# Input gradient of a strided convolution: even and odd positions as matmul groups in the last five chunks, shared products split once more, instruction order written out as a list

## The chip, the cores and the metric

One core of one Trainium2 chip runs the whole kernel in one launch. The metric is the device time of one execution in microseconds (us); lower is better. The core has five engines: PE (TensorE, matmuls; its weight loads are shown as PEld), DVE (VectorE), ACT (ScalarE), POOL (GpSimd) and SP (SyncE, which here issues nearly all DMAs). Each engine runs its own instructions in the order in which they are written, and waits on semaphores for the others.

## The reference

Forward: a convolution with stride 2 and 31 taps over `x` (2 x 16000 x 256), with a 256 x 256 matrix per tap, then a normalisation over time per batch and channel, scale and shift, and a GELU. The kernel returns the output and all four gradients for a given `grad_out` (2 x 7985 x 256), in bf16:

```python
s = 2
L = (T - K) // s + 1                       # 7985
h = jnp.einsum('blc,cd->bld', x[:, 0:s * L:s, :], w[0])
for i in range(1, K):
    h = h + jnp.einsum('blc,cd->bld', x[:, i:i + s * L:s, :], w[i])
mu = jnp.einsum('bld->bd', h)[:, None, :] / L
var = jnp.einsum('bld->bd', (h - mu) ** 2)[:, None, :] / L
h = (h - mu) / jnp.sqrt(var + 1e-5)
return _gelu(h * gn_gamma[None, None, :] + gn_beta[None, None, :])

_out, _vjp = jax.vjp(_f, x, w, gn_gamma, gn_beta)
return (_out, *_vjp(grad_out))
```

The change lies in the gradient with respect to `x`: the gradient `dl` of `h`, convolved with the transposed and reversed taps.

## The kernel before, in words

**Stages.** The forward convolution of the two batches (stages F0 and F1) comes first, then the input gradient (G0 and G1) with the elementwise gradient of the GELU beside it, and last the weight gradient (W). Each stage is a long stream of matmuls on PE, with bf16 operands in SBUF (one big tile, `arena`) and fp32 sums in PSUM (`ps`, eight banks, used as four pairs).

**Products saved by differences.** All three convolutions replace products by sums. Positions and taps are dealt out by their remainders; a pair of outputs that would need four block products gets by with three, one of which (on a difference or sum of inputs, with a difference or sum of taps) is shared by both outputs. This is done three times over: a branch `br` in {B, A, C} and a leaf `lf` in {B, A, C} name the two outer levels, nine leaves in all, and inside a leaf a third level shares one product between the output halves `e` = 0 and 1.

**The input gradient.** It goes through eight chunks t = 4b + c (batch b, chunk c) of 2048 positions. In a chunk DVE forms the differences on which the leaves work (`g_sums`, line 1278: `first` for the branch, `second` for its leaves A and C, `third` for the two inputs of the unshared products). PE then runs units, one for each half chunk `pr` and branch: six units to a chunk. A unit owns two PSUM pairs, `px` and `pt`:

- `g_three_b` (line 1351): the shared product of leaf B, 4 matmuls of 512 columns into one bank of `px`; ACT copies it to the other bank (line 1359).
- `g_outer` (line 1361), in the last five chunks alone (t = 3 to 7, `GO`): the shared products of leaves A and C, 4 matmuls each, into the two banks of `pt`.
- `g_three_ac` (line 1369) for leaf B: 8 matmuls added to `px`.
- `g_seed` (line 1381): ACT keeps `pt` in SBUF (`GTB`, by `keep`, line 839), and one DVE addition of 128 x 2048 (line 1393) writes the start values of both `pt` and `px`: leaf B's sum plus the shared product of A, or of C.
- `last(A)` and `last(C_)`, run during the next unit: 8 matmuls each by `g_three_ac`, and `g_evac` (line 1395), which for branches A and C adds the kept sums of branch B on DVE (line 1403) into the output tile `HO`, and for branch B keeps them on ACT (line 839). SP stores `HO` in runs of 4096 bytes.

That is 36 matmuls of 512 columns to a unit in the last five chunks. `W2DO` and `W2DC` hold the tap sums for `g_outer`; `w2_outer` forms them during t = 2.

**The gradient of h.** `e_load` (line 1199) loads two tiles of 512 KB (`dyd` and `hd`) per chunk and channel half, `e_comp` (line 1207) scales and adds them. The scaling is on DVE for t = 3, 4, 5 (lines 1214 and 1216) and on ACT for t = 6, 7 (lines 1221 and 1223), the addition on DVE (line 1225). ACT then spreads the sum over the planes of a tile `ET`, of which there are two (line 1234).

**For the weight gradient**, `dl_turn` (line 1262) transposes each of the nine leaves of a chunk by two DMA transposes from SP (line 557) into one of four small tiles `DNO`, and POOL stores them to DRAM (`dld`, line 552). `weight_grad` (line 1664) loads them back (`d_tile`), and subtracts some of them (line 1706) ahead of its first matmuls (line 1540).

**What sets the order.** The helpers do not emit; each records an operation with its engine and what it reads and writes. `Plan.order` gave every operation a due time (from a table of leads and a finer table by part), and `Plan.listing` ran a model of the engines and queues over them; the recorded operations were then emitted in the order of the model's start times (`emit`, line 461). Each engine's own program order comes from that list.

Of the kernel before, what the change touches and what calls it, by code (L numbers as in the profile page):

```python
# [38 lines left out]
class Plan:  # L39

    def __init__(self, tc):
# [7 lines left out]
        self.look = 13  # L51
        self.pads = (3122.5, 3149.5, 2842.0)
        self.lead = {
            "F0 f_evac last": 5.0,
            "F0 f_mm f_leaf": -288.0,
            "F0 f_mm f_outer": -149.5,
            "F0 f_mm f_three_ac": -4.5,
            "F0 f_mm f_three_b": -5.5,
            "F0 f_mm pe_turn": -527.0,
            "F0 f_outer forward": -46.0,  # L60
            "F0 f_seed forward": -48.5,
            "F0 f_three_b forward": -129.5,
            "F0 keep f_evac": 35.5,
            "F0 load conv_stem_kernel": -15.5,
            "F0 load f_evac": 42.5,
            "F0 tt f_sums": -120.5,
            "F0 tt second": 20.5,
            "F0 tt third": -36.0,
            "F0 turn w2_part": -3.0,
            "F0 turn x_load": -8.5,  # L70
            "F0 ve f_seed": -122.5,
            "F0 ve_neg f_seed": 49.0,
            "F0 w_sub f_first": -76.5,
            "F0 w_sum w2_part": -13.5,
            "F1 f_evac last": -106.5,
            "F1 f_mm f_leaf": -335.0,
            "F1 f_mm f_outer": 74.0,
            "F1 f_mm f_three_ac": -8.5,
            "F1 f_mm f_three_b": -75.5,
            "F1 f_three_b forward": -73.0,  # L80
            "F1 gelu_unit gelu_batch": -2.0,
            "F1 load gelu_unit": 23.0,
            "F1 load out0_store": 15.0,
            "F1 tt f_sums": -79.5,
            "F1 tt gelu_unit": -49.5,
            "F1 tt second": -38.0,
            "F1 tt third": -225.5,
            "F1 turn gelu_batch": 56.0,
            "F1 turn gelu_unit": -12.5,
            "F1 turn x_load": 35.5,  # L90
            "F1 w_sub f_again": 4.5,
            "G0 e_comp e_load": 0.5,
            "G0 g_evac last": 1.5,
            "G0 g_mm g_leaf": -24.5,
            "G0 g_mm g_outer": 22.0,
            "G0 g_mm g_three_ac": -0.5,
            "G0 g_mm g_three_b": -7.0,
            "G0 g_three_b input_grad": 4.5,
            "G0 gelu_unit gelu_batch": -7.0,
            "G0 keep g_evac": -281.0,  # L100
            "G0 keep g_seed": -15.0,
            "G0 load dl_turn": 2.5,
            "G0 load e_load": 41.0,
            "G0 load g_evac": 23.5,
            "G0 load gelu_unit": -7.0,
            "G0 spread e_comp": -1.0,
            "G0 tiny elem_finalize": -1.0,
            "G0 tt first": -111.5,
            "G0 tt second": -4.5,
            "G0 tt third": -12.5,  # L110
            "G0 turn dl_turn": 3.5,
            "G0 turn gelu_batch": -12.0,
            "G0 w_sum load_w2": -53.0,
            "G0 w_sum w2_outer": -11.5,
            "G1 cp e_comp": 7.0,
            "G1 e_comp e_load": 12.0,
            "G1 g_mm g_outer": -15.0,
            "G1 g_mm g_three_ac": -8.5,
            "G1 g_mm g_three_b": -35.0,
            "G1 g_seed input_grad": 8.5,  # L120
            "G1 g_three_b input_grad": -11.0,
            "G1 keep g_evac": -1.0,
            "G1 keep g_seed": -108.5,
            "G1 load dl_turn": 11.0,
            "G1 load e_load": -6.0,
            "G1 load g_evac": 14.5,
            "G1 spread e_comp": -5.5,
            "G1 tt second": -16.0,
            "G1 tt third": -128.0,
            "G1 turn dl_turn": 4.0,  # L130
            "G1 zero e_comp": -6.0,
            "W keep w_keep": -3.0,
            "W keep weight_grad": -12.5,
            "W leaf_d weight_grad": 0.5,
            "W load d_tile": -54.0,
            "W load out0_late": 115.0,
            "W load w_done": -7.5,
            "W load w_emit": 28.0,
            "W load weight_grad": 2.0,
            "W load x_more": -9.0,  # L140
            "W load x_raw": 1.0,
            "W pair_d weight_grad": 1.5,
            "W pair_x weight_grad": 1.5,
            "W turn out0_late": -21.0,
            "W ve w_done": -11.0,
            "W ve weight_grad": -25.0,
            "W w_add weight_grad": 2.5,
            "W w_add x_more": 1.5,
            "W w_add x_tile": 29.5,
            "W w_both weight_grad": 11.0,  # L150
            "W w_emit w_done": 13.0,
            "W w_emit weight_grad": -261.0,
            "W w_mm w_leaf": -10.0,
            "W w_pairs weight_grad": -112.5,
        }
        self.spare = {k + " dl_turn": 3.0 for k in ("G0 turn", "G0 load", "G1 turn", "G1 load")}
        self.room, self.mixed = 2048.0, 2.2
        self.overlap = {"DVE": 0.084, "ACT": 0.1}
        self.fine = {
            "F0 f_evac last": {0: -191.0, 1: -57.0, 3: -4.0},  # L160
            "F0 f_mm f_outer": {0: 138.5, 2: 14.0},
            "F0 f_mm f_three_ac": {0: -41.0, 1: -74.0, 2: -68.0, 3: -25.5},
            "F0 f_mm f_three_b": {2: 96.5, 3: 55.0},
            "F0 f_mm pe_turn": {0: -106.0},
            "F0 f_outer forward": {0: 69.5},
            "F0 f_seed forward": {0: -15.0, 3: -58.5},
            "F0 keep f_evac": {1: -5.5, 2: -40.5, 3: -32.5},
            "F0 load f_evac": {0: -85.5, 3: 8.5},
            "F0 load put": {1: 170.5, 3: 1.0},
            "F0 load_gb conv_stem_kernel": {1: -70.0},  # L170
            "F0 tt f_sums": {1: 46.0, 3: 20.0},
            "F0 tt second": {0: 77.0, 1: -78.0, 2: 2.0, 3: -60.0},
            "F0 tt third": {0: 60.5, 1: -127.0, 2: 39.0, 3: -34.5},
            "F0 turn w2_part": {1: 3.0, 3: -18.0},
            "F0 turn x_load": {0: 87.0, 1: 94.0, 3: 29.5},
            "F0 ve_neg f_seed": {0: 232.5, 2: 9.0},
            "F0 w_sub f_first": {0: 132.0},
            "F0 w_sum w2_part": {0: 47.5, 1: 26.5, 2: 10.0, 3: 9.5},
            "F1 f_mm f_leaf": {1: 73.0},
            "F1 f_mm f_outer": {3: -293.5},  # L180
            "F1 f_mm f_three_ac": {3: -2.0},
            "F1 f_mm f_three_b": {3: -106.0},
            "F1 gelu_unit gelu_batch": {0: -7.0, 4: 15.5, 6: 23.5},
# [153 lines left out]
    def listing(self, due, succ):  # L337
# [14 lines left out]
        air = []  # L352
# [1516 lines left out]
```

## Time and profile before

| | before |
|---|---|
| median of 3 runs (lowest to highest) | 1144.24 us (1144.07 to 1147.97) |
| span of the profiled execution | 1144.1 us |
| PE busy | 1120.0 us, 98%, 7652 matmuls |
| PE weight loads busy | 748.4 us, 65% |
| DVE busy | 997.0 us, 87% |
| ACT busy | 530.1 us, 46% |
| POOL busy | 126.3 us, 11% |

The profile is of one execution, whose span is within 0.2 us of the median; nothing else of it lies outside the span. The tables by stretch (called windows here) give each engine's busy time between two points, counted from the span's start, the count of instructions in brackets, the mean TensorE clock that was granted (PEclk, 1.00 is full) and the mean load of the sixteen DMA engines. In timelines and groups, the bracket at the end of a row is the idle time of that engine just before it, and what ended it. Rows of `PE` are matmuls, `PEld` their weight loads, `SPq` DMAs as SP issues them.

By the lines of the matmuls, the input gradient runs from about 412 to 829 us and the weight gradient from there on; the first `g_seed` addition of the last five chunks (line 1393) begins at 595 us, the last one at 823 us.

### The profile page before, as it was taken

What the parts mean: (1) busy time and instruction counts of PE and PEld (TensorE: products, weight loads), DVE (VectorE), ACT (ScalarE), POOL (GpSimd) and SP (SyncE); (2) the same over time, 40 slices, a digit from 0 to 9 for tenths busy, and PEclk for the clock granted to TensorE, in tenths of its full rate; (3) what the DMA queues carried; (4) which work ended last, traced back from release to release, by engine and by line L of the source; (5) the groups of instructions that cost most, each with busy time, mean ns of one, the idle gap of its engine ahead of it and who ended that gap; (6) DMA issues with size and microseconds to landing.
All of it is one profiled execution on the core that took longest, in us unless ns stands there. A gap on an engine that the chain in (4) does not pass through costs nothing.

```text
span 1144.1 us, 18907 instructions
## 1 busy us (share of the span) xinstructions
PE 1120.0 (98%) x7652; PEld 748.4 (65%) x7652; DVE 997.0 (87%) x931; ACT 530.1 (46%) x814; POOL 126.3 (11%) x221
## 2 busy tenths in 40 slices
PE   6999999999999999999999989999999999999998
PEld 4888899877777874444444434444488766666785
DVE  7998787798989997999899877967799998788995
ACT  1353454768777588888744454732212212111200
POOL 0000000000000002232223233132200000000000
PEclk9999999999999999999999999999999999999999
DMA  9476657769786599999979787695898825999564
GB/s 221 76 190 114 168 159 149 169 177 203 192 213 151 198 362 263 278 302 247 236 204 242 168 193 162 198 235 140 262 322 259 292 72 200 347 332 310 181 200 130
DMA packets 348249, 243.57 MB, mean 213 GB/s; under 512 B 233819, under 2 KB 317409, under 8 KB 345985
## 3 DMA queue, kind: packets, MB, share of 16 engines
q1 hardware_dynamic: 341057, 223.47, 72.8%
q0 software_dynamic: 7104, 18.89, 6.0%
q8 instruction: 60, 0.98, 0.4%
q14 instruction: 28, 0.23, 0.1%
HBM read 106.24 MB, written 80.25 MB: 163 GB/s over the span
## 4 chain that ended last, share of the span: by engine, by line
PE 78%; DVE 12%; DMA 3%; issue 3%; ACT 2%; SPq 2%; DVEq 0%; ACTq 0%
PE ps L744 32%; PE ps L1540 25%; PE ps L1332 21%; DVE ps L1393 2%; DVE arena L1403 2%; SPq L552 1%; DVE arena L1285 1%; DVE arena L1119 1%; DVE arena L686 1%; DVE arena L702 1%; DVE arena L1225 1%; SPq L557 1%; DMA arena<-vl 1%; DMA arena<-in_x_dram 1%; DMA arena<-dyd 1%
## 5 line engine op out<-in xcount | busy, mean ns | idle before, releaser
L744 PE MATMUL ps<-arena 128*128 128x256 bf16 (+4 forms) x3460 | 407.9, 281 | 10.0 <-DMA arena<-in_x_dram 5.8
L1332 PE MATMUL ps<-arena 128*128 128x512 bf16 x1872 | 403.9, 377 | 7.8 <-ACT ps L1359 4.8
L744 PEld LDWEIGHTS <-arena 128*128 128x128 bf16 x3460 | 338.0, 98 | 79.8 <-DMA arena<-in_x_dram 6.1
L1332 PEld LDWEIGHTS <-arena 128*128 128x128 bf16 x1872 | 183.6, 98 | 227.3 <-issue 15.5
L1540 PE MATMUL ps<-arena 128*128 128x256 bf16 (+1 forms) x2320 | 308.9, 296 | 2.4 <-DVE arena L1706 1.5
L1540 PEld LDWEIGHTS <-arena 128*128 128x128 bf16 x2320 | 226.8, 98 | 84.5 <-issue 1.9
L839 ACT ACTIVATE arena<-ps 128x1024 f32<-128x1024 f32 x109 | 110.7, 1022 | 259.7 <-PE ps L1540 86.6
L702 DVE TENSOR_TENSOR arena<-arena 128x2064 bf16<-128x2064 bf16 (+8 forms) x125 | 155.4, 1268 | 31.9 <-PE ps L744 31.4
L552 POOL DMA_DIRECT2D dld<-arena x144 | 104.3, 726 | 252.4 <-DMA arena<-arena 232.4
L1119 DVE TENSOR_TENSOR arena<-arena 128x2048 bf16<-128x2048 bf16 (+1 forms) x80 | 95.7, 1196 | 8.3 <-ACT arena L1113 5.0
L1285 DVE TENSOR_TENSOR arena<-arena 128x1032 bf16<-128x1032 bf16 (+1 forms) x126 | 88.7, 726 | 8.0 <-PE ps L1332 4.1
L1393 DVE TENSOR_TENSOR ps<-ps,arena 128x2048 f32<-128x2048 f32 x30 | 68.9, 2296 | 29.0 <-PE ps L1332 17.6
L1505 DVE TENSOR_TENSOR arena<-arena 128x4096 bf16<-128x4096 bf16 (+1 forms) x50 | 87.2, 1779 | 6.0 <-DMA arena<-in_x_dram 5.8
L1403 DVE TENSOR_TENSOR arena<-ps,arena 128x1024 bf16<-128x1024 f32 x64 | 76.8, 1217 | 12.7 <-PE ps L1332 12.5
L859 ACT ACTIVATE arena<-ps 128x512 bf16<-128x512 f32 (+1 forms) x64 | 37.1, 580 | 52.6 <-PE ps L744 52.1
L1642 ACT COPY ps<-ps 128x256 f32<-128x256 f32 x54 | 19.3, 359 | 84.1 <-PE ps L1540 82.9
L561 POOL MEMSET arena<- 128x128 bf16 (+11 forms) x40 | 8.5, 243 | 430.1 <-DVE arena L702 140.0
L1359 ACT COPY ps<-ps 128x512 f32<-128x512 f32 x48 | 27.8, 580 | 41.7 <-PE ps L1332 41.7
L814 ACT ACTIVATE arena<-ps 128x512 f32<-128x512 f32 x56 | 29.7, 598 | 36.1 <-DVE ps L824 20.6
L1711 DVE TENSOR_TENSOR arena<-arena 128x4608 bf16<-128x4608 bf16 x16 | 40.6, 2556 | 4.7 <-PE ps L1540 4.7
L1626 DVE TENSOR_TENSOR arena<-arena 128x2048 bf16<-128x2048 bf16 x36 | 43.0, 1224 | 1.2 <-PE ps L1540 1.1
L780 ACT ACTIVATE ps<-ps 128x256 f32<-128x256 f32 x72 | 26.6, 370 | 32.8 <-PE ps L744 31.6
(81 smaller groups left out, 717.7 us busy)
## 6 DMA issues: line engine op xcount, KB each, us to landing
arena<-in_x_dram SPq DMA_DIRECT2D x28, 1024.0 KB
dld<-arena POOLq DMA_DIRECT2D x144, 128.0 KB, 4.0
out_dram<-arena SPq DMA_DIRECT2D x35, 512.0 KB
arena<-hd SPq DMA_DIRECT2D x32, 512.0 KB
arena<-in_x_dram SPq DMA_DIRECT2D x26, 512.0 KB
arena<-dld SPq DMA_DIRECT2D x18, 640.0 KB
arena<-dld SPq DMA_DIRECT2D x18, 576.0 KB
vl<-arena SPq DMA_DIRECT2D x36, 256.0 KB
```

The lines of the kernel that those rows point to most:

```text
L552: lambda: e.dma_start(out=out, in_=in_), dma=np_ * ns / 16e3 * 1.03, ns=ns, tp=SH[pk], slack=slack)
L702: lambda: nc.vector.tensor_tensor(out=o, in0=a, in1=b, op=ALU.add))
L744: yield nc.tensor.matmul(ps[:, dh, cs], lhsT=wt, rhs=mv, start=s0, stop=False, skip_group_check=True)
L839: lambda: nc.scalar.activation(out=out, in_=ps, func=ACT.Copy, scale=scale))
L1119: add("DVE", dve(nf), [o], [a, b_], lambda: V.tensor_tensor(out=o, in0=a, in1=b_, op=op))
L1285: lambda: nc.vector.tensor_tensor(out=o, in0=a, in1=b, op=ALU.subtract))
L1332: yield nc.tensor.matmul(ps[:, e, 0:wide], lhsT=lt, rhs=mv, start=s0, stop=False, skip_group_check=True)
L1393: lambda: nc.vector.tensor_tensor(out=o, in0=x, in1=g, op=ALU.add))
L1403: lambda: nc.vector.tensor_tensor(out=ho[:, :, k, :], in0=ps[:], in1=g, op=ALU.add))
L1505: add("DVE", dve(o.free_size()), [o], [a, b], lambda: nc.vector.tensor_tensor(out=o, in0=a, in1=b, op=ALU.add))
L1540: yield nc.tensor.matmul(ps[:, s, c0:c1], lhsT=lt, rhs=mv, start=s0, stop=False, skip_group_check=True)
L1626: add("DVE", dve(2048), [o], [u, v], lambda o=o, u=u, v=v: nc.vector.tensor_tensor(out=o, in0=u, in1=v, op=ALU.subtract))
```

## The change

**The last five chunks (t = 3 to 7) are computed in other groups.** A unit was one branch of a run of 128 neighbouring output positions (`pr`). Now it is one branch of every second position: `s` = 0 the even ones, `s` = 1 the odd ones. The weight operand of such a matmul is read with a step of two elements. The loops are now chunk, branch, `s`; before they were chunk, `pr`, branch.

**The shared products of leaves A and C are split a fourth time.** With the two taps w0 and w1 of a shared product and its input P, the even positions need P[2k] w1 + P[2k+1] w0 and the odd ones P[2k+1] w1 + P[2k+2] w0. `g_common` computes P[2k+1] (w0 + w1) once for both (2 matmuls a leaf, with the new tap sums `W4`), ACT keeps it in SBUF (`GTM`), and for the odd positions ACT writes it back to PSUM; `g_apart` adds the difference P[2k] - P[2k+1], or P[2k+1] - P[2k+2], times one tap (2 matmuls a leaf and `s`; one of the taps is negated beforehand). The differences are one new DVE operation per chunk and branch (`fourth`). For a chunk and branch this is 4 + 8 matmuls where `g_outer` had 16.

**What goes with it.** `g_seed` makes two DVE additions of 128 x 1024 in place of one of 128 x 2048. The gradient of h is written straight into planes (`EP`, `P3`): for t = 4 to 7 it is loaded in four quarters of 256 KB per tile through one pair of buffers (`EGP`), scaled on ACT and added on DVE by two instructions; the ACT copies of `e_comp` are gone there. `EP` and the branch tiles `SA` and `SC` exist once. `DNO` has three tiles for these chunks, not four. The transposes of a branch's leaves follow that branch, so those of branch C come last. The output is stored for each branch and `s`, in runs of 1024 bytes.

**The order is a list.** `Plan.order`, `Plan.listing` and their tables are gone; `SEQUENCE` names all 3414 recorded operations in the order in which they are emitted. It is another order in all stages, the forward and the weight gradient among them, whose operations are the same as before.

```diff
+SEQUENCE = (
+    1, 9, 11, 0, 3, 12, 2, 10, 21, 13, 4, 5, 8, 14, 7, 6, 15, 16, 37, 33, 34, 40, 30, 31,
...
+)
...
     def emit(self):
         pin = self.tc.keep_in_program_order
-        for i in self.order():
...
+        for i in SEQUENCE:
...
+    EP, P3 = sb(182016, 3, 2, 2, EM), [sb(o, 2, 2, EM) for o in (165376, 188224)]
+    EGP = [sb(o, 4, HM) for o in (86016, 88064)]
...
     def e_load(b, c):
+        if 4 * b + c > 2:
+            e_planes(b, c)
+            return
...
+    def e_planes(b, c):
...
+        for dh in range(2):
...
+            for e in range(2):
+                eg, eh = (v[:, e] for v in EGH[dh]) if t == 3 else EGP
+                gv, hv = (v.rearrange("p k f -> p (k f)") for v in (eg, eh))
+                if t > 3:
+                    for v, d in ((hv, h_d[b][c]), (gv, dy_d[b][c])):
+                        load(v, d[:, 2048 * dh + 1024 * e:2048 * dh + 1024 * e + 1024], 1 << 18, 2048, "SP")
+                e_scale(t, gv, hv, s4, s5, s6)
+                o, i = EP[:, :, dh, e, 2:2 + wd], [v[:, 1:4, 0:wd] for v in (eg, eh)]
+                e_add(o, *i)
+                w3 = wd + (wd < HM and e == 0)
+                o = p3[:, dh, 1 - e, 1 + e:1 + e + w3]
+                e_add(o, eg[:, 0, 0:w3], eh[:, 0, 0:w3])
...
+        def fourth(br):
+            v = GLS[place(br)][:, :, :, 1]
+            tt(GDE[:, :, :, 0:257], v[:, :, :, 0:257], v[:, :, :, 1:258])
...
+    def step_of(s):
+        return lambda q: slice(s + q, s + q + 2 * P - 1, 2)
...
+    def g_common(pt, br, pl, lf):
+
+        w4, k = W4[MIR[br], MIR[lf]], 0 if lf == A else 1
+        jobs = [(k, 512, pl[1][:, dh, 1:2 * P:2], w4[:, dh, :], dh == 0) for dh in range(2)]
+        g_mm(pt, jobs, [pt[:, k]], [w4, pl[1]])
+
+    def g_apart(pt, br, lf, s):
+
+        wd, k = (W2DO if lf == A else W2DC)[MIR[br]], 0 if lf == A else 1
+        jobs = [(k, 512, GDE[:, k, dh, s:s + 2 * P - 1:2], wd[:, dh, 1 - s, :], False) for dh in range(2)]
+        g_mm(pt, jobs, [pt[:, k]], [wd[:, :, 1 - s], GDE[:, k], pt[:, k]])
...
         keep(GTB.rearrange("p k f -> p (k f)"), flat2(pt))
...
-        add("DVE", dve(2048, 1), [pt[:], px[:]], [px[:], GTB],
-            lambda: nc.vector.tensor_tensor(out=o, in0=x, in1=g, op=ALU.add))
+        for k, ps in ((0, pt), (1, px)):
...
+            add("DVE", dve(1024, 1), [ps[:]], [px[:], GTB[:, k]],
+                lambda ps=ps, g=g: nc.vector.tensor_tensor(out=ps[:], in0=px[:], in1=g, op=ALU.add))
...
+        for t in range(3, 8):
...
+            for br in ORDER:
+                for s in range(2):
+                    at = step_of(s)
+                    px, pt = slots4(i)
+                    if s == 0:
+                        us = {B_: third(br, B_)}
+                    g_three_b(px, br, B_, planes(br, B_), at)
+                    if s == 0:
+                        second(br, A)
+                        second(br, C_)
+                        fourth(br)
+                    if s == 0:
+                        for lf in (A, C_):
+                            g_common(pt, br, planes(br, lf), lf)
+                    last(A)
...
+                    if s == 0:
+                        keep(GTM.rearrange("p k f -> p (k f)"), flat2(pt))
+                    else:
+                        keep(flat2(pt), GTM.rearrange("p k f -> p (k f)"))
+                    for lf in (A, C_):
+                        g_apart(pt, br, lf, s)
+                    g_three_ac(px, br, B_, us[B_], at)
...
+                        last(C_)
+                    if s == 0:
+                        us[A], us[C_] = third(br, A), third(br, C_)
+                    g_seed(px, pt, True)
...
-        if (pr, br) == (1, B_):
+        if 4 * b + c < 3 and (pr, br) == (1, B_):
             dl_turn(b, c, leaf)
+        if 4 * b + c > 2 and pr == 0:
+            dl_turn(b, c, leaf, (br,))
```

**Where instructions stand now.** ACT, before, where the gradient of the third chunk of batch 1 (t = 6) is loaded. Line 1359 copies a leaf B product, line 839 keeps a PSUM pair in SBUF, lines 1221 and 1223 scale a 512 KB load of `hd` and of `dyd`, line 1234 spreads the sum:

```order
L839 ACTIVATE arena<-ps 128x1024 x3
L1359 COPY ps<-ps 128x512
L1223 ACTIVATE arena<-arena,stats 128x1024 x2
L1221 ACTIVATE arena<-arena,stats 128x1024 x2
L1359 COPY ps<-ps 128x512
L839 ACTIVATE arena<-ps 128x1024
L1234 COPY arena<-arena 128x3x256 x2
L1234 COPY arena<-arena 128x256 x2
L839 ACTIVATE arena<-ps 128x1024 x2
```

And ACT now, where that of the second chunk of batch 1 (t = 5) is loaded. Line 1264 is the copy of a leaf B product, line 643 is `keep` (`arena<-ps` keeps a PSUM pair, `ps<-arena` writes `GTM` back), lines 1062 and 1064 scale a 256 KB load of `hd` and of `dyd`:

```order
L643 ACTIVATE arena<-ps 128x1024 x3
L1062 ACTIVATE arena<-arena,stats 128x1024
L1064 ACTIVATE arena<-arena,stats 128x1024
L643 ACTIVATE arena<-ps 128x1024 x2
L643 ACTIVATE ps<-arena 128x1024
L1264 COPY ps<-ps 128x512
L643 ACTIVATE arena<-ps 128x1024
L1264 COPY ps<-ps 128x512
L1062 ACTIVATE arena<-arena,stats 128x1024
L643 ACTIVATE arena<-ps 128x1024
```

The scalings of a 512 KB pair of loads stood together, four in a row; now those of each 256 KB pair stand apart, twice as often, with the writes of `GTM` between them.

SP, before, at the end of the input gradient. `in_x_dram` and `dld` are loads for the weight gradient, the transposes are those of `dl_turn`, `out_dram` are stores:

```order
L557 DMA_TRANSPOSE arena<-arena 128x4x128 x11
L552 DMA arena<-in_x_dram 128x8x512 x2
L552 DMA arena<-dld_0_80 128x2304
L557 DMA_TRANSPOSE arena<-arena 128x4x128 x2
L552 DMA out_dram<-arena 128x2048 x2
L552 DMA arena<-dld_0_89 128x2304
L552 DMA arena<-dld_0_80 128x2560
L552 DMA arena<-dld_0_89 128x2560
```

And SP now, at the same place (line 349 is the transpose, line 344 any other DMA):

```order
L349 DMA_TRANSPOSE arena<-arena 128x4x128 x4
L344 DMA out_dram<-arena 116x4x512
L349 DMA_TRANSPOSE arena<-arena 128x4x128
L344 DMA arena<-dld_2_82 128x2560
L349 DMA_TRANSPOSE arena<-arena 128x4x128
L344 DMA out_dram<-arena 116x4x512
L349 DMA_TRANSPOSE arena<-arena 128x4x128
L344 DMA arena<-dld_0_89 128x2560
L349 DMA_TRANSPOSE arena<-arena 128x4x128
L344 DMA arena<-dld_0_89 128x2304
```

In the list before, all but two of the last chunk's transposes are issued ahead of the first `dld` loads. In the new list the last four transposes shown stand singly between these loads and the last stores. `dld_0_89` holds transposed leaves of batch 1 for the first matmuls of the weight gradient.

More of the change, by code (lines that the diff above doesn't have):

```diff
@@ L50, in __init__ @@
         self.hold = -1
[L51 to L155, printed above, removed]
@@ L461, in emit @@
     def emit(self):
         pin = self.tc.keep_in_program_order
[L463 removed]
+        place = {i: k for k, i in enumerate(SEQUENCE)}
+        assert len(place) == len(self.ops)
+        assert all(place[p] < place[i] for i, o in enumerate(self.ops) for p in o["preds"])
+        for i in SEQUENCE:
             r = self.ops[i]["fn"]()
@@ L1243, in e_comp, with e_add, e_edge @@
+    def e_add(o, a, b_):
+        add("DVE", dve(o.free_size()), [o], [a, b_], lambda: nc.vector.tensor_tensor(out=o, in0=a, in1=b_, op=ALU.add))
+    def e_edge(b, c):
+        et = ET[(4 * b + c) % 2]
         if c == 0:
```

540 lines of the change are left out of this document (190 added, 350 removed), and 145 rows, old and new, of tables (MIR, SEQUENCE).

## The prediction

> **What bounds the kernel now.** I read the page's totals first, then the chain that ended last.
>
> ```profile
> span 1144.1 us, 18907 instructions
> ...
> PE 1120.0 (98%) x7652; PEld 748.4 (65%) x7652; DVE 997.0 (87%) x931; ACT 530.1 (46%) x814; POOL 126.3 (11%) x221
> ...
> PE 78%; DVE 12%; DMA 3%; issue 3%; ACT 2%; SPq 2%; DVEq 0%; ACTq 0%
> ```
>
> PE is busy for 98% of the span, so only fewer matmuls or fewer gaps can shorten it. A table of windows, cut at the stages and at PE's gaps, says where the 24.1 us without a matmul are (us, PE, PEld, DVE, ACT, POOL with counts, granted clock, DMA load, GB/s).
>
> ```profile
> 41.00:408.00 367.00, 366.54 (x3130) 305.53 (x3128) 320.53 (x313) 222.03 (x401) 5.54 (x14) 1.00 0.72 176
> 408.00:590.00 182.00, 179.25 (x893) 87.17 (x891) 168.05 (x193) 146.58 (x186) 47.09 (x77) 1.00 1.01 270
> 590.00:660.00 70.00, 67.50 (x312) 30.33 (x310) 64.14 (x77) 30.12 (x41) 21.11 (x34) 1.00 0.85 205
> 660.00:670.00 10.00, 8.02 (x30) 3.33 (x30) 6.80 (x5) 6.00 (x9) 6.02 (x9) 0.83 1.05 173
> 670.00:822.00 152.00, 151.82 (x710) 69.24 (x709) 115.64 (x104) 64.22 (x78) 42.20 (x70) 1.00 0.75 192
> 822.00:850.00 28.00, 25.81 (x205) 19.92 (x204) 28.00 (x26) 4.29 (x9) 1.44 (x2) 1.00 1.06 362
> 850.00:1140.30 290.30, 289.69 (x2149) 209.80 (x2147) 259.22 (x184) 49.65 (x80) 0.53 (x1) 1.00 0.73 233
> ```
>
> The last five chunks of the input gradient, which the change rewrites, fill 590 to 822. From 670 on PE is busy for 151.82 of 152 us: there a matmul that goes takes its full time out of the span, unless a new wait puts it back. The one bad spot is 660 to 670, with 30 matmuls in 10 us and a granted clock of 0.83. Of the 24.1 us, 13.4 lie at the start and the end of the program. The forward stage (41 to 408) loses 0.46 us, the weight gradient (850 on) 0.6 us. Another order has nothing to win there; I count it at 0, with 1.5 us to either side.
>
> The sum is made against the profiled execution, 1144.1 us, which is the median (1144.24) within 0.2.
>
> **Part by part: fewer matmuls.** The price of one matmul of 512 columns is read from a stretch of PE's timeline without a gap.
>
> ```profile
> 779.71 21.99 PE L1332 MATMUL ps<-arena 128*128 128x512 bf16 x102
> ```
>
> 21.99 / 102 = 0.2156 us. For each chunk and branch `g_outer` had 16 matmuls, `g_common` and `g_apart` have 4 + 8 = 12. Five chunks, three branches: 15 x 4 = 60 matmuls fewer, 1080 become 1020. Check: 1080 x 0.2156 = 232.8 us, and the windows from 590 to 822 are 232. So -60 x 0.2156 = **-12.9 us**. The Trainium skill's "TensorE: Matmul & The Clock Gate" (section "Back-to-back issue gap") gives about 131 ns for a 512-column matmul in a sustained stream; by it 60 would be worth 7.9 us and the sum below 1138; the trace shows 216 ns, and it decides.
>
> **The stall at 657.** The timelines of SP, ACT and PE in order of time:
>
> ```profile
> 650.93 0.53 SPq L552 DMA_DIRECT2D arena<-dyd  x1
> ```
> ```profile
> 657.00 2.19 ACT L1223 ACTIVATE arena<-arena,stats 128x1024 bf16<-128x1024 bf16 x2 [4.94 <-DMA arena<-dyd]
> ...
> 661.36 0.57 ACT L1359 COPY ps<-ps 128x512 f32<-128x512 f32 x1
> ```
> ```profile
> 661.98 10.26 PE L1332 MATMUL ps<-arena 128*128 128x512 bf16 x39 [3.05 <-ACT ps L1359]
> ```
>
> ACT waits 4.94 us for a `dyd` load that landed 6.07 us after its issue, and the leaf B copy (line 1359) stands behind four scalings. PE loses 3.05 us, and then matmuls at the lower clock: 30 in 660 to 670, where a full rate gives 46. 16 x 0.2156 = 3.4 us in that window, plus 1.1 us of the gap before 660: about 4.5 us. The new order has no such row of four, and this load goes in quarters. I take the whole **-4.5** (bounds -4.5 and 0).
>
> **The new loads.** Sixteen pairs of 256 KB per quarter take the place of 512 KB ones, all through one pair of buffers `EGP`, so a load can be issued only when the last pair's additions are done. The two later waits of this kind:
>
> ```profile
> 711.59 0.52 SPq L552 DMA_DIRECT2D arena<-dyd  x1
> ...
> 727.70 0.33 SPq L552 DMA_DIRECT2D arena<-dyd  x1
> ```
> ```profile
> 716.37 2.19 ACT L1223 ACTIVATE arena<-arena,stats 128x1024 bf16<-128x1024 bf16 x2 [3.17 <-DMA arena<-dyd]
> ...
> 732.43 2.19 ACT L1223 ACTIVATE arena<-arena,stats 128x1024 bf16<-128x1024 bf16 x2 [1.33 <-DMA arena<-dyd]
> ```
>
> Here the pair lands 4.78 and 4.73 us after issue, ACT waits 3.17 and 1.33 us, and PE none (151.82 of 152). In the new list 15 to 27 matmuls, about 4.2 us on average, stand between such a load and its scaling, so with 4.8 to 6.1 us ACT waits 0.6 to 1.9 us a pair: 9 to 29 us over 15 pairs (the first has a free buffer) if PE paid it all, nothing if the cover of 716.37 holds. Waits of up to 3.17 us cost nothing there, so I stay near that end: 0.2 us a pair, **+3.0** (0 to +23). Behind a waiting scaling on ACT stand the leaf B copy, the `GTM` moves and the keeps; PE waits for the first two. "DMA: Bandwidth & Descriptors" of the Trainium skill (section "Anatomy of one DMA — SWDGE (gpsimd) path") counts 2.0 us fixed and the bytes at 436 GB/s: an estimate by it for two 256 KB loads is 3.2 us, this term would be 0 and the sum 1130. That section is about another queue, and no run here shows a 256 KB load of this kind.
>
> **The `GTM` chain, and the entry.**
>
> ```profile
> L839 ACT ACTIVATE arena<-ps 128x1024 f32<-128x1024 f32 x109 | 110.7, 1022 | 259.7 <-PE ps L1540 86.6 <-PE ps L1332 59.4 <-DVE arena L1569 58.4
> L839 ACT ACTIVATE ps<-ps 128x1024 f32<-128x1024 f32 x23 | 23.2, 1007 | 17.0 <-PE ps L1332 5.4 <-PE ps L1540 5.2 <-DVE arena L1403 3.5
> L1234 ACT COPY arena<-arena 128x768 bf16<-128x768 bf16 x32 | 25.6, 828 | 5.7 <-DVE arena L1225 5.5
> L1221 ACT ACTIVATE arena<-arena,stats 128x1024 bf16<-128x1024 bf16 x8 | 9.5, 1230 | 0.1
> ```
>
> For the even positions PE runs `g_common`, then mostly 8 other matmuls (8 x 0.2156 = 1.72 us), then `g_apart` into the same banks; ACT must have kept them by then (1.02 us). That leaves 0.70 us for handovers and for whatever ACT is doing; a scaling of 1.1 to 1.2 us in the way breaks it. In one group only 4 matmuls (0.86 us) stand between. At the entry into t = 3 the list leaves two distances about 1.4 and 1.5 us short. I take **+2.5** for all (0 to +5). ACT itself has room: 30 `GTM` moves add 30 x 1.02 = 31 us and the scalings about 19, the 40 spreads that go take some 24 away, on (30.12 + 6.00 + 64.22) of 232 us.
>
> **DVE.**
>
> ```profile
> L1285 DVE TENSOR_TENSOR arena<-arena 128x1032 bf16<-128x1032 bf16 x118 | 79.2, 692 | 5.4 <-PE ps L1332 3.9 <-DMA arena<-arena 0.7
> L1403 DVE TENSOR_TENSOR arena<-ps,arena 128x1024 bf16<-128x1024 f32 x64 | 76.8, 1217 | 12.7 <-PE ps L1332 12.5
> L1393 DVE TENSOR_TENSOR ps<-ps,arena 128x2048 f32<-128x2048 f32 x30 | 68.9, 2296 | 29.0 <-PE ps L1332 17.6 <-ACT arena L839 11.0 <-ACT ps L1359 0.4
> L824 DVE TENSOR_TENSOR ps<-ps,arena 128x1024 f32<-128x1024 f32 x28 | 34.0, 1226 | 2.2 <-PE ps L1540 2.2
> L1225 DVE TENSOR_TENSOR arena<-arena 128x2048 bf16<-128x2048 bf16 x16 | 19.5, 1219 | 2.2 <-ACT arena L1221 2.1
> ```
>
> Per chunk: three `fourth` at 0.692 add 2.1 us; twelve seeds at 1.226 for six at 2.296 add 0.9; the `e` path in pieces, with DVE's scalings gone, saves about 0.7. Together +2.3. DVE was busy 186.6 of the 232 us, 37.3 a chunk; it becomes 39.6, against a PE time per chunk of 204 x 0.2156 = 44.0: 90%, no bound by itself, cost 0 in the forecast. In 408 to 590 DVE was busy at 92% and PE still at 98.5%.
>
> **The border to the weight gradient.**
>
> ```profile
> 816.42 2.60 SPq L557 DMA_TRANSPOSE arena<-arena  x2
> ```
> ```profile
> 822.32 1.44 POOL L552 DMA_DIRECT2D dld<-arena  x2 [10.83 <-DMA arena<-arena]
> ```
> ```profile
> dld<-arena POOLq DMA_DIRECT2D x144, 128.0 KB, 4.0
> ```
> ```profile
> 842.05 8.13 PE L1540 MATMUL ps<-arena 128*128 128x256 bf16 x73 [1.50 <-DVE arena L1706]
> ```
>
> Here 2.19 us are lost already (822 to 850), most of it at 842.05. The way of a leaf into the weight gradient is: transposes 2.6, until the store's issue 3.3 (819.0 to 822.3), the issue 0.7, its landing 4.0, and the load back at the 4.7 to 6.1 us of `dyd`: 15 to 17 us. In the new list branch C's transposes come last, singly among the loads, and about 75 matmuls (16.2 us) stand between, before about 30 us. So it comes out about even: **+0.7** (0 to +5).
>
> Sum: 1144.1 - 12.9 - 4.5 + 3.0 + 2.5 + 0.7 = 1132.9, **1133 us**; its own range, with the middle of the bounds, 1128 to 1138.
>
> **Rivals.** *No new waits, 1125.* Without the 6.2 us of new waits it is 1126.7, and the rest of the 2.5 us lost in 590 to 660 can go too. For it: the list leaves most users some distance. Against: two terms are short by the rows. 0.12.
>
> *DVE sets the pace, about 1142.* The means of the rows add up to 43.2 us a chunk; at the 92% that is the highest share in any such window this is 47.0, 3.0 over PE's 44.0: +15 us in five chunks, 1148 at most; a third to two thirds of it lies between 1138 and 1143. Against it: three line 1285 sums back to back take 1.90 us, not 3 x 0.692, so the means count overlap twice.
>
> ```profile
> 646.75 1.90 DVE L1285 TENSOR_TENSOR arena<-arena 128x1032 bf16<-128x1032 bf16 x3
> ```
>
> 0.15.
>
> *Slower: late loads fall through to PE, about 1154.* The place is ACT, at each scaling of an `EGP` quarter; the copies behind it now have a slack of 0.7 us, not the 3.17 of before. At 1.5 us for each of 15 pairs this is +23 in place of +3.0. It decides once a pair lands about 7 us after its issue, since the list gives 4.2 and ACT's slack some 2 to 3. For it: one landing was 6.07, and SP has transposes queued ahead of the loads. Against: half the bytes. 0.11.
>
> *Slower: strided weight loads, 1213.* 1020 loads now read every second element.
>
> ```profile
> L1332 PEld LDWEIGHTS <-arena 128*128 128x128 bf16 x1872 | 183.6, 98 | 227.3 <-issue 15.5 <-DVE arena L1285 0.2
> ```
>
> A load of 98 ns hides under a matmul of 216. Only beyond that does it cost: at three times 98, 294 - 216 = 78 ns x 1020 = 80 us. No row of before has a strided load. "SBUF — State Buffer" of the Trainium skill (section "Door 1: The DMA port swizzle") says that a stride is free up to 8 bf16 elements, a 16-byte line; no run yet shows it. 0.02.
>
> *The change does not do what it says* (a stage elsewhere loses by the new order what this one wins): the windows of the other stages are full, so little speaks for it; about 1142. 0.02.
>
> **How the numbers follow.** Forecast 0.58, the better case 0.12: faster by over 0.5% (5.7 us, about what a measurement of this kernel can tell from no change), that is below 1138.4: 0.70. DVE and the other stages: same, 0.17. Late loads and strided loads: slower, 0.13. The likeliest is 1133. The range leaves out late and strided loads and the outer edge of the DVE case (its ends 1138 to 1148): 1124 to 1145.
>
> **What would show it.** Right: 7592 matmuls; the late chunks' matmuls 13 us shorter in sum at 0.216 each; no gap of 3 us with a low clock; ACT waiting 0.5 to 2 us on most quarters with PE idle not over some 6 us in the stage; weight loads still near 98 ns. Wrong: PE's gaps ended by ACT (`GTM`, leaf B copy) of 1 us and more a unit; DVE over 95% with PE waiting on seeds or differences; a gap of several us ahead of the weight gradient; matmuls longer than 0.216 us.

## The result, and the profile after

The changed kernel takes 1174.93 us (median of 4 runs, 1173.89 to 1176.20) beside 1144.84 us for the kernel before: a ratio of 1.0259, 95% interval 1.0246 to 1.0273. It is slower by about 30 us. The forecast was 1133 us, with a range of 1124 to 1145; slower had a chance of 0.13.

The page of the profile after; its span is 1173.3 us, 29.2 more than before:

```profile
span 1173.3 us, 18859 instructions
...
PE 1113.2 (95%) x7539; PEld 744.9 (63%) x7592; DVE 1008.2 (86%) x1013; ACT 560.8 (48%) x826; POOL 137.2 (12%) x212
```

The 60 matmuls are gone (7592 weight loads for 7652; of the matmuls 53 records are missing). PE is busy for 6.8 us less, not 12.9, and has no matmul for 60.1 us where it was 24.1. The windows, with the columns as before, say where:

```profile
408.00:590.00 182.00, 171.81 (x830) 83.35 (x846) 163.96 (x198) 142.11 (x180) 56.48 (x79) 0.99 1.02 265
590.00:660.00 70.00, 62.60 (x276) 27.86 (x281) 61.56 (x90) 42.10 (x47) 16.69 (x27) 0.98 0.64 151
660.00:670.00 10.00, 9.95 (x48) 4.66 (x48) 8.83 (x12) 5.48 (x7) 2.57 (x4) 1.00 0.78 118
670.00:822.00 152.00, 142.99 (x647) 64.97 (x659) 127.61 (x159) 86.43 (x95) 45.95 (x64) 0.97 0.85 211
822.00:850.00 28.00, 17.96 (x80) 8.56 (x81) 16.70 (x15) 4.24 (x5) 4.33 (x6) 0.92 0.81 138
```

Before, PE lacked 2.8, 2.5, 2.0, 0.2 and 2.2 us in these five. Now it lacks 10.2, 7.4, 0.1, 9.0 and 10.0. PE's timeline has the larger gaps one by one (between 400 and 900 us, no other is longer than 1.7 us):

```profile
414.69 0.38 PE L1231 MATMUL ps<-arena 128*128 128x512 bf16 x1 [4.02 <-ACT arena L1099]
416.15 1.06 PE L1231 MATMUL ps<-arena 128*128 128x512 bf16 x2 [1.08 <-ACT arena L668]
...
609.24 13.95 PE L1231 MATMUL ps<-arena 128*128 128x512 bf16 x55 [3.25 <-DVE arena L1179]
...
680.54 145.10 PE L1231 MATMUL ps<-arena 128*128 128x512 bf16 x651 [8.05 <-ACT arena L643]
...
837.47 2.34 PE L1231 MATMUL ps<-arena 128*128 128x512 bf16 x7 [2.38 <-DVE ps L1308]
...
853.07 24.20 PE L1497 MATMUL ps<-arena 128*128 128x256 bf16 x208 [9.44 <-DMA arena<-dld]
882.11 28.51 PE L1497 MATMUL ps<-arena 128*128 128x256 bf16 x240 [4.84 <-DVE arena L1583]
```

Together 33.1 us: the entry into the input gradient (two rows), one wait at t = 3, one on a late load at 680, and three around the border to the weight gradient. The gap at 680, followed back along ACT and SP:

```profile
677.31 1.24 ACT L1062 ACTIVATE arena<-arena,stats 128x1024 bf16<-128x1024 bf16 x1 [9.39 <-DMA arena<-hd]
```
```profile
665.42 0.48 SPq L344 DMA_DIRECT2D out_dram<-arena  x1
665.95 4.69 SPq L349 DMA_TRANSPOSE arena<-arena  x1
670.75 1.15 SPq L344 DMA_DIRECT2D arena<-hd  x1
```

ACT stands 9.39 us before a `hd` quarter. On DVE, the buffer's last use by the quarter before:

```profile
662.07 0.55 DVE L1067 TENSOR_TENSOR arena<-arena 128x768 bf16<-128x768 bf16 x1
```

It was free at 662.6. The load was issued at 670.75, 8 us later: SP had two more transposes to finish first, until 665.4, then came an output store, and right behind it a transpose that took 4.69 us to issue. The border shows the same pair, store and then a slow transpose, ahead of the `dld` loads on which the weight gradient waits:

```profile
834.73 0.43 SPq L344 DMA_DIRECT2D out_dram<-arena  x1
835.33 5.55 SPq L349 DMA_TRANSPOSE arena<-arena  x1
845.15 0.34 SPq L344 DMA_DIRECT2D arena<-dld  x1
```

Elsewhere in the same kernel transposes behind an output store take a usual time, two of them 2.76 us:

```profile
686.00 0.53 SPq L344 DMA_DIRECT2D out_dram<-arena  x1
686.64 2.76 SPq L349 DMA_TRANSPOSE arena<-arena  x2
```

What differs is the store. Those at 665 and 834 belong to the last chunk of a batch and have 116 partitions; that at 686 has 128. The windows in which the packets of the stores issued at 654.49, 665.42 and 686.00 moved (the last two columns are the DMA engines' load and GB/s):

```profile
656.70:664.40 7.70, 7.65 (x37) 3.50 (x36) 7.70 (x12) 5.11 (x6) 2.57 (x4) 1.00 0.73 91
666.50:674.80 8.30, 5.99 (x29) 2.85 (x29) 2.65 (x3) 1.02 (x1) 1.44 (x2) 1.00 0.83 102
687.10:688.90 1.80, 1.80 (x10) 0.82 (x9) 0.50 (x1) 1.80 (x3) 1.17 (x2) 1.00 1.03 318
```

The single DMA packets of the trace, counted for some stores (in flight = sum of the packets' times over the time from the first one's start to the last one's end):

```
kernel, store issued, partitions    packets  from..to         mean ns  in flight
after, 665.42, 116                  464      666.47..674.85   58       3.2
after, 834.73, 116                  464      836.55..843.94   51       3.2
after, 686.00, 128                  512      687.07..688.91   51       14.1
```

A packet of 1024 bytes takes as long in the one as in the other, 50 to 60 ns. But the store of 116 partitions has only three to four packets in flight, and lasts 7 to 8 us in place of 1.8. Theory T1: these eight stores, four in chunk t = 3 and four in t = 7, run on about four of the sixteen DMA engines, and what is queued with them comes late. The rival T2: single load buffers, late transposes and the written order are the cause, whatever a store takes.

### The profile page after: what moved, and what is told of

Read it like the earlier page. It is cut to its first block, busy times and chain, and to the rows that moved or that the text cites. A ratio compares the mean times of both kernels' runs of the same rounds, so it can differ in the third digit from the quotient of the medians.

```text
span 1173.3 us, 18859 instructions
## 1 busy us (share of the span) xinstructions
PE 1113.2 (95%) x7539; PEld 744.9 (63%) x7592; DVE 1008.2 (86%) x1013; ACT 560.8 (48%) x826; POOL 137.2 (12%) x212
## 5 line engine op out<-in xcount | busy, mean ns | idle before, releaser
L1231 PE MATMUL ps<-arena 128*128 128x512 bf16 (+1 forms) x1774 | 393.6, 380 | 29.7 <-ACT arena L643 9.7
L1497 PE MATMUL ps<-arena 128*128 128x256 bf16 (+1 forms) x2305 | 312.8, 298 | 16.5 <-DMA arena<-dld 9.4
L643 ACT ACTIVATE arena<-ps 128x1024 f32<-128x1024 f32 x124 | 125.1, 1020 | 255.4 <-PE ps L1497 104.7
L506 DVE TENSOR_TENSOR arena<-arena 128x2080 bf16<-128x2080 bf16 (+6 forms) x125 | 155.4, 1267 | 30.7 <-PE ps L548 30.4
L1308 DVE TENSOR_TENSOR ps<-ps,arena 128x1024 f32<-128x1024 f32 x60 | 72.6, 1227 | 12.5 <-ACT arena L643 8.5
L1179 DVE TENSOR_TENSOR arena<-arena 128x1032 bf16<-128x1032 bf16 (+1 forms) x110 | 72.4, 693 | 4.7 <-PE ps L1231 3.9
L353 POOL MEMSET arena<- 128x128 bf16 (+9 forms) x31 | 8.7, 335 | 420.3 <-DVE arena L506 260.4
L1318 DVE TENSOR_TENSOR arena<-ps,arena 128x1024 bf16<-128x1024 f32 x40 | 48.5, 1219 | 7.1 <-PE ps L1231 3.4
L908 ACT ACTIVATE arena<-arena,stats 128x1024 bf16<-128x1024 bf16 (+1 forms) x32 | 37.6, 1210 | 15.1 <-DMA yd<-arena 9.4
L913 DVE SCALAR_TENSOR_TENSOR arena<-arena 128x2048 bf16<-128x2048 bf16 (+1 forms) x16 | 35.8, 2238 | 6.0 <-ACT arena L910 5.9
```

The costliest lines, as they stand in the source:

```text
L506: lambda: nc.vector.tensor_tensor(out=o, in0=a, in1=b, op=ALU.add))
L643: lambda: nc.scalar.activation(out=out, in_=ps, func=ACT.Copy, scale=scale))
L1179: lambda: nc.vector.tensor_tensor(out=o, in0=a, in1=b, op=ALU.subtract))
L1231: yield nc.tensor.matmul(ps[:, e, 0:wide], lhsT=lt, rhs=mv, start=s0, stop=False, skip_group_check=True)
L1308: lambda ps=ps, g=g: nc.vector.tensor_tensor(out=ps[:], in0=px[:], in1=g, op=ALU.add))
L1318: lambda: nc.vector.tensor_tensor(out=ho[:, :, k, :], in0=ps[:], in1=g, op=ALU.add))
```

## The experiments

The expectations quoted here count the runs in another way: their first run is experiment 1, their sixth is experiment 5 with the changed operations, their tenth is experiment 9.

**1. Split the eight stores.** One DMA of 116 partitions becomes two, of 112 and 4:

```diff
-    def load(out, in_, nbytes, run, eng="SP", slack=None, own=False):
+    def load(out, in_, nbytes, run, eng="SP", slack=None, own=False, cuts=(0, None)):
...
-            lambda: e.dma_start(out=out, in_=in_), dma=...
+            lambda: (e.dma_start(out=out[a:z], in_=in_[a:z]) for a, z in zip(cuts, cuts[1:])), dma=...
...
-            load(dst, ho[0:r]..., r * 4096, 1024, "POOL", slack=60.0)
+            load(dst, ho[0:r]..., r * 4096, 1024, "POOL", slack=60.0, cuts=(0, 112, r) if c == 3 else (0, None))
```

> The changed kernel; each of the eight output stores with 116 partitions (last chunk of a batch) is issued as two DMAs, of 112 and of 4 partitions; nothing else differs. Theory T1 (the 116-partition stores flow through only about four of the sixteen DMA engines, 6 to 8 us each instead of 1.5 to 2.7, and hold up the transposes and loads behind them on SP; the late load at 680 and the wait ahead of the weight gradient follow from that): 20 to 28 us less, 1147 to 1155 us, the stall of 8.05 us gone, that of 9.44 us at most a third. Theory T2 (single load buffers, late transposes and the written order are the cause, whatever a store takes): within 5 us of the changed kernel, 1170 to 1175.

Measured: 1149.31 us, ratio to before 1.0040 (1.0022 to 1.0059). That is 25 to 26 us less than the changed kernel, and nothing but the issue of eight stores differs. Its SP timeline at the same chunk, and its window of one split store:

```profile
646.45 1.02 SPq L344 DMA_DIRECT2D out_dram<-arena  x2
647.68 4.59 SPq L349 DMA_TRANSPOSE arena<-arena  x3
```
```profile
647.80:649.80 2.00, 1.89 (x10) 0.78 (x8) 2.00 (x4) 0.38 (x1) 1.45 (x2) 1.00 1.02 293
```

Three transposes now take what one took, and the store's 464 packets pass in 2.0 us with 12.6 in flight. On PE the gap at 680 is gone; what is left of the others:

```profile
414.55 0.59 PE L1231 MATMUL ps<-arena 128*128 128x512 bf16 x1 [4.02 <-ACT arena L1099]
...
605.55 12.41 PE L1231 MATMUL ps<-arena 128*128 128x512 bf16 x55 [2.53 <-DVE arena L1179]
...
826.18 24.53 PE L1497 MATMUL ps<-arena 128*128 128x256 bf16 x208 [3.68 <-DMA arena<-dld]
851.28 1.91 PE L1497 MATMUL ps<-arena 128*128 128x256 bf16 x16 [0.57 <-DVE arena L1583]
```

T1 holds. Some 4 to 5 us over the kernel before remain, which T2 would put down to the order and the buffers; experiments 5 and 6 take up the order. The border's wait is a little more than the third that was expected, 3.68 of 9.44.

**2. The opposite: make twelve more stores slow.** Stores of 128 partitions in t = 4 to 6 become 124 and 4:

```diff
-... cuts=(0, 112, r) if c == 3 else (0, None))
+... cuts=(0, r - 4, r) if b == 1 and c < 3 else (0, None))
```

> The changed kernel; the twelve stores of 128 partitions of chunks t = 4 to 6 are issued as 124 and 4 partitions, those of 116 are left as they are. T1: if the number of DMA engines follows from the number of partitions (124 and 116 are multiples of 4 alone, 128 of 16), each of the twelve now takes 6 to 8 us: 20 to 45 us more, 1195 to 1220 us, with new stalls between 685 and 815. T2: twelve more issues of 0.4 us off the critical path, within 3 us.

Measured: 1220.10 us, ratio 1.0645 (1.0618 to 1.0672), 45 us more than the changed kernel, at the upper end of what T1 gave. Waits of PE, summed (us, times, longest):

```profile
PE ps L1231 <- ACT arena L643: 25.8, 6, 9.6
PE ps L1231 <- ACT ps L643: 12.8, 6, 4.9
```

The same bytes, with four partitions of 128 in a DMA of their own; the store issued at 687.94 moved its 512 packets from 688.96 to 698.28, 3.1 in flight. So neither the 1024-byte runs nor the amount is at fault. The Trainium skill, "DMA: Bandwidth & Descriptors" (section "Why a DMA increments its semaphore by 16 and not by 1"), says that a DMA is dealt to the largest number of engines, at most 16, that divides the slowest dimension of both its sides. By that 116 and 124 give 4 engines, 112 and 128 give 16. The trace agrees in the stores counted here: 3.1 to 3.2 packets in flight for the former, 12.6 to 14.1 for the latter.

**3. The same split in the kernel before**, whose last half chunks store 104 partitions (now 96 and 8):

> The kernel before; its stores of 104 partitions (last half chunk of a batch) are issued as 96 and 8 partitions; the order is the same. T1: a store of 104 partitions uses eight DMA engines; the transpose behind it at 644.78 took 4.16 us and so delayed the load on which ACT waited 4.94 us; the 3.05 us stall of PE at 661.98 goes, 2 to 5 us less, 1139 to 1143 us. T2: that load was late by the order, within 1 us of before.

Measured: 1144.66 us, ratio 0.9997 (0.9985 to 1.0009): nothing. T1's expectation for this kernel missed. A pair of these stores had about 10 packets in flight (208 of 4096 bytes in 5.2 us). Eight engines, on which the expectation rested, is wrong by the rule of the Trainium skill just named: 13 divides 104. The split does not remove the stall at 657:

```profile
660.98 1.43 PE L1332 MATMUL ps<-arena 128*128 128x512 bf16 x3 [2.21 <-ACT ps L1359]
```

**4. The 60 matmuls alone**, left out of the kernel before:

```diff
-            for e, wide, lt, mv, s0 in jobs:
+            for e, wide, lt, mv, s0 in jobs[:len(jobs) - left_out]:
...
-        g_mm(pt, jobs, [pt[:, k]], [wd, pl[1]])
+        g_mm(pt, jobs, [pt[:, k]], [wd, pl[1]], 1)
```

> The kernel before; the last of the four matmuls of each shared product of leaves A and C is left out (60 of 512 columns), everything else and the order as before, so one of four products of these sums is missing. If PE bounds the late chunks, as the prediction had it: 11 to 14 us less, 1131 to 1134 us. If DVE, ACT or the loads set the pace there: under 6 us less.

Measured: 1139.86 us, ratio 0.9949 (0.9928 to 0.9970): 3 to 8 us less by the interval, 4.2 by the medians. That is short of the 11 to 14 us of the first expectation and mostly within the second's "under 6". Its profiled execution is 8.5 us shorter than that of before. PE's group of 512-column matmuls in both profiles, with the idle time ahead of them and what ended it:

```profile
L1332 PE MATMUL ps<-arena 128*128 128x512 bf16 x1730 | 387.6, 379 | 12.7 <-ACT ps L1359 4.3 <-DVE ps L1393 3.0 <-ACT arena L839 1.1
```

```profile
L1332 PE MATMUL ps<-arena 128*128 128x512 bf16 x1828 | 402.7, 380 | 7.8 <-ACT ps L1359 4.8 <-ACT arena L839 1.1 <-DVE ps L1393 1.0
```

The first is without the 60 matmuls, the second before: 12.7 us of idle time for 7.8, and 3.0 of it on line 1393 for 1.0. With fewer matmuls PE now reaches the DVE seeds before they are done. So in the old order PE was not the only bound: between a third and three quarters of the 12.9 us is given back to other waits.

**5. and 6. Both kernels in another order.** Now the operations were left alone and the lists written anew for both, by the same search, which moves each operation earlier or later among those of its engine as long as nothing that it depends on is passed. The changed kernel has the split stores.

```diff
-SEQUENCE = (
-    1, 9, 11, 0, 3, 12, 2, 10, 21, 13, 4, 5, 8, 14, 7, 6, 15, 16, 37, 33, 34, 40, 30, 31,
...
+SEQUENCE = (
+    1, 2, 11, 40, 33, 34, 35, 39, 41, 30, 31, 32, 37, 36, 38, 12, 46, 42, 43, 44, 21, 51, 52, 53,
...
```

> The changed kernel with the split stores of 112 and 4 partitions and, in all stages, another order of the same operations, chosen so that loads, sums and transposes come earlier ahead of their users. Theory A (what is left over the kernel before is the written order: waits of 4.0 and 0.9 us at the entry into the input gradient, 1.2 and 2.5 at t = 3, 3.7 at the border, 1 to 1.2 in the weight gradient, some 18 us with the lower clock after them): 1128 to 1138 us. Theory B (the changed operations themselves, more and smaller ones on ACT and DVE, cost what the 60 matmuls save): 1143 to 1150 us whatever the order.

> The kernel before, operations unchanged (its stores of 104 partitions as 96 and 8), in an order chosen in the same way. It shows what the order alone is worth, so that the sixth and this run differ by the change's operations: theory A: 1132 to 1142 us here and 8 to 14 us more than the sixth run; theory B: within 4 us of the sixth run, or less than it.

Measured: the changed operations 1130.34 us, ratio 0.9879 (0.9859 to 0.9899); the operations of before 1140.96 us, ratio 0.9957 (0.9942 to 0.9973). The page of the former:

```profile
span 1126.1 us, 18868 instructions
...
PE 1101.4 (98%) x7538; PEld 741.1 (66%) x7592; DVE 1013.4 (90%) x1013; ACT 562.7 (50%) x826; POOL 132.4 (12%) x212
```

Theory A holds: both times lie in its ranges. The order alone gives the changed operations 18 us (0.9879 for 1.0040), and those of before 5. So the new list cost some 13.5 us against the planner's, beside the stores. With orders made by the same search the changed operations are worth 9 to 11 us (0.9879 for 0.9957; 10.6 by the medians). That both orders are equally good for their kernels is assumed, not shown. The first of these two kernels beats both kernels of this case.

**7. That order with the eight stores whole.**

> The sixth run's order with the eight stores of 116 partitions left whole. If these stores cost what they block on SP's queue in any order (T1): 15 to 35 us more than the sixth run. If only the changed kernel's own order let them through to PE: within 5 us of it.

Measured: 1152.45 us, ratio 1.0065 (1.0042 to 1.0087), 22 us more than with split stores. Its waits of PE:

```profile
PE ps L1231 <- DVE arena L1318: 8.5, 2, 7.5
PE ps L1231 <- ACT arena L643: 6.2, 2, 5.9
```

And one of DVE's:

```profile
DVE arena L1318 <- DMA out_dram<-arena: 17.5, 4, 8.6
```

The stores cost about as much in an order that leaves few other waits, and here much of it goes by one more way: line 1318 writes the output tile, and waits until the last store has read it. In the changed kernel's own order this way shows once, at the border, ahead of PE's wait of 2.38 us at 837.47:

```profile
832.78 1.22 DVE L1318 TENSOR_TENSOR arena<-ps,arena 128x1024 bf16<-128x1024 f32 x1 [3.31 <-DMA out_dram<-arena]
```

**8. Contiguous weight operands** in all late matmuls:

```diff
-        return lambda q: slice(s + q, s + q + 2 * P - 1, 2)
+        return lambda q: slice(s + q, s + q + P)
...
```

The operands of `g_common` and `g_apart` lose their step in the same way.

> The sixth run, but the weight operand of all late matmuls is read without a step (128 neighbouring columns, so the sums are over wrong positions). If strided weight loads cost nothing: within 2 us of the sixth run, weight loads 98 to 99 ns in both. If they cost something on PE: 4 us less or more.

Measured: 1129.03 us, ratio 0.9856 (0.9841 to 0.9870), 1.3 us from the run with strides, with intervals that overlap. Weight loads with the step, and then without:

```profile
L1231 PEld LDWEIGHTS <-arena 128*128 128x128 bf16 x1812 | 177.2, 98 | 217.6 <-issue 9.7 <-DVE arena L1179 2.1 <-DVE arena L1129 0.7
```
```profile
L1231 PEld LDWEIGHTS <-arena 128*128 128x128 bf16 x1812 | 177.0, 98 | 220.2 <-issue 12.2 <-DVE arena L1179 3.1 <-DVE arena L1129 0.7
```

Here a step of two elements costs nothing that can be measured.

**9. The whole stores on POOL's queue**, in the changed kernel's own order (the store call gets `own=c == 3`):

> The changed kernel with its eight stores of 116 partitions whole, but issued from POOL's queue instead of SP's. If such a store does its harm by keeping the transposes and loads behind it on SP's queue waiting: 1145 to 1160 us, transposes behind former store places back at 1.2 us. If it does it by occupying DMA engines or memory for every queue: 1168 us or more.

Measured: 1177.89 us, ratio 1.0273 (1.0245 to 1.0301): as slow as on SP. The expectation from SP's queue missed. SP's transposes behind the old places are slow still:

```profile
647.30 27.04 SPq L349 DMA_TRANSPOSE arena<-arena  x10
```

Within this row the first six took 1.2 to 1.4 us each to issue, the last four, from 657 on, 2.6 to 3.9, though no store stands between them on their queue: POOL issued its stores at 654.80 and 665.19. Between 668 and 672 the packets of POOL's queue had 3.2 to 4.0 in flight. That could also have been another harm, since the small stores of transposed leaves now follow the big ones on POOL. So:

**10. The same, split.**

> The changed kernel with its eight stores of 116 partitions issued from POOL's queue, as in the tenth run, and split into 112 and 4 partitions, as in the first. The tenth run (1178 us) left two readings. If a whole store does its harm by keeping few DMA engines busy, on whichever queue it stands: 1147 to 1157 us here, as in the first run. If the tenth run only put another harm in its place (the small stores of transposed leaves that follow on POOL's queue come late, whole store or not): 1165 us or more.

Measured: 1147.35 us, ratio 1.0031 (1.0011 to 1.0052), as in the first experiment. The 116 packets of the first split store on POOL's queue passed in 3.2 us with 11.3 in flight. On either queue the split is worth 25 to 28 us by the ratios: what counts is how many packets of a store can be in flight, which fits the number of DMA engines over which it is dealt, and not which engine issues it.

The packets also show what waited. In the changed kernel, behind the store issued at 665.42, SP's queue started no 256-byte packet, of which the transposes consist, from 666.43 to 670.52. Of the 256 packets of 2048 bytes of the `hd` and `dyd` loads issued at 670.75 and 672.01, 250 started after the store's last packet had ended at 674.85. Why they wait while few packets are in flight isn't settled, since the trace doesn't name a packet's engine.

**11. The quarter loads left out**, all but the first two, with split stores. The load call is made to record nothing to run, its place in the order stays.

> The changed kernel with split stores (as the first run, 1149 us), and of the 32 quarter loads of dyd and hd only the first two are made; the scalings go on over the same two buffers, so the gradient of h is wrong from t = 4 on. The prediction counted +3.0 us (0 to 23) for waits on these loads. If they cost that once the stores are out of the way: 1143 to 1148 us. If they still are the main loss: 1140 us or less. If they are hidden: within 1.5 us of the first run.

Measured: 1147.28 us, ratio 1.0020 (1.0008 to 1.0031), 2 us below the first experiment with intervals that overlap. The loads cost 0 to 5 us once the stores are out of the way; whether they cost about the 3.0 that the prediction counted or almost nothing can't be told apart.

## Why the prediction was wrong, point by point

- **What failed: the output stores were not costed.** The part on the change went through matmuls, loads, `GTM`, DVE and the border, and had no term for the stores, which the sum so put at nothing, though the change alters their form too: from 128 or 104 partitions with runs of 4096 bytes to 128 or 116 with runs of 1024. The eight of 116 partitions cost 25 us (experiment 1), about as much in another order (22 us, experiment 7), and as much on the other queue (9, 10).
- **The new loads, +3.0.** Not contradicted once the slow stores are gone (0 to 5 us, experiment 11). The rival "late loads fall through to PE" named the place, ACT ahead of the scaling of a quarter, and the wait came there, twice, with 8.05 and 1.64 us, not on each of 15 pairs. The load ahead of the 8.05 us landed 6.6 us after its issue, near the 7 that the rival named; but the larger part was an issue that came 8 us after its buffer was free, and the working had counted from the issue on only. Both delays lay behind output stores. So this rival had the direction right, but not the cause.
- **The border, +0.7 (0 to +5).** It was 9.44 and 4.84 us on PE, against 1.50 before. In experiment 1 it is 3.68 and 0.57. The chain of the working, transposes to load, left out what stands on SP between its links: a transposed leaf's last transpose was issued at 833.45, the load at 845.15, behind a store and a transpose of 5.55 us.
- **"Another order has nothing to win" elsewhere, 0 with 1.5 to either side.** It had something to lose. By experiments 1, 5 and 6 the new list cost 13.5 us against the planner's, over all stages. The entry into the input gradient, for one, waits 4.02 us at 414 and about 1 us behind it, with and without slow stores, and not in experiments 5 and 6. The entry into t = 3 (3.25 us) is within the +2.5 (0 to +5) of its term.
- **The saving, -12.9.** The mechanism was right: 7592 matmuls, 0.216 us each. The changed operations as a whole were worth 9 to 11 us in the searched order; the 60 matmuls alone brought 3 to 8 in the old one. "A matmul that goes takes its full time out" was read from a stretch in which PE was full; with fewer matmuls DVE comes due in places.
- **The stall at 657, -4.5.** In experiment 1, where only stores are split, there is no gap of more than 0.5 us between 620 and 800. The stall did go, and in the changed kernel the new one at 680 outweighed it. That the quarters did it is not shown: the operations of before in another order (experiment 6) have no gap of more than 0.9 us there either.
- **DVE as the pace, strided loads.** Neither: in experiment 1 DVE is busy for 137.93 of 152 us from 670 to 822 (91%, where the working had 90%) and PE for 149.56, the seeds take 1.226 us as counted, and the strides cost nothing (experiment 8).

In sum, by ratios to before: changed operations -9 us, the list's order against the planner's +13.5, eight stores +25. The three are differences taken one after the other and so make up the 30 us by construction; that each would be as large without the other two is not shown.

## What to carry to other kernels

When a change alters the shape of a DMA, cost the DMA as a term of its own, even a store for which nothing seems to wait: look at how many packets are in flight, and give its slowest dimension a multiple of 16, splitting off the rest. When a new kernel comes with a new order, try both kernels in orders made in the same way before judging the operations. And follow a chain of transfers through everything that is queued between its links, not only through its own durations.

## What the runs showed of the hardware

One store of 464 KB, 116 partitions in 1024-byte runs, takes 5.9 to 8.4 us, one of 512 KB and 128 partitions 1.5 to 3 us; 112 and 4 partitions together take 2 to 3 us (experiment 1). A transpose behind the former needed 4.5 to 5.7 us to issue, behind the latter 1.2 to 2.6, in the changed kernel. PE also lost to the clock: the same 1730 matmul records of 512 columns took 391.6 us in the changed kernel and 386.9 with split stores. The granted clock was 0.92 in the window of the border (822 to 850) and 0.97 in the one that holds the stall at 680.
